# Longer query fetches, merged output stores and column-paired MLP products in a fused retention and MLP kernel

## The chip, the cores and the metric

The kernel runs on one core of one Trainium2 chip. The metric is the device time of one execution, in microseconds, given as the median of several runs. A run is called slow when it lies over 1.5% above the fastest of the same kernel; ratios leave slow runs out.

## The reference, cut to what matters

```python
# q, k, v: (8, 8, 576, 64) float32; w_in: (512, 2048); w_out: (2048, 512)
scores = (q @ k.transpose(0, 1, 3, 2)) / sqrt(64)
Dmat   = where(i >= j, gamma[h] ** (i - j), 0)          # decay, causal
attn   = (scores * Dmat) @ v                             # (8, 8, 576, 64)
x      = attn.transpose(0, 2, 1, 3).reshape(4608, 512)
h      = x @ w_in
out    = (h * clip(h + 3, 0, 6) / 6) @ w_out             # (4608, 512)
```

## The kernel before

The sequence is cut into chunks of 128 rows (four of each of eight batches) and four tail chunks, numbered 0 to 35 in order of use. The queries, keys and values of a chunk are loaded by SyncE, scaled to 16 bits by GpSimd or VectorE, and the scaled queries and keys are transposed by a DMA that ScalarE issues. TensorE then makes the chunk's scores and its part of x. When the chunks of a batch are done, the MLP runs on that block of 512 rows: TensorE makes an up product, ScalarE an activation `u` from it, VectorE `g`, and TensorE the down products, which from block 1 on are seven products in place of eight. So while block n goes through the MLP, the chunks of block n+1 go through attention, on all engines at once.

The order of everything is one long string that is worked off token by token: `l20` loads chunk 20, `c20.0g` scales its queries on GpSimd (`v` is VectorE), `x20` transposes, `s20` and `o20` are scores and output, `u3.5` is an up product and its activation, `P3.4` a down product. Each engine's list of instructions follows the order of this string, and in the trace of the kernel before each engine runs through its list in order, going by source lines: TensorE's 3,695 matmuls, VectorE's 341 instructions and SyncE's 180 DMAs without exception, and ScalarE's 294 instructions but for five transposes that begin one or two places early.

```python
COL_UP, COL_DOWN = (5, 6, 8, 7), (4, 5, 6, 8, 7)   # blocks in column pairs

def load(c, only=None):                              # three loads a chunk
    ...
    nc.sync.dma_start(st[:, ix, :, :],               # runs of 256 bytes
        src[b, :, t * P:(t + 1) * P, :].rearrange("h s d -> s h d"))

def xpose(c):
    qt = work.tile([P, 8, P], FP16, tag="qkT", bufs=4, name="qkT")
    nc.scalar.dma_start_transpose(qt, qk.rearrange("p a h d -> p (a h d)"))

def mul(ps, lhs, rhs, start, stop, halves=True):
    if not halves:
        nc.tensor.matmul(ps, lhs, rhs, ...)          # full, 128 columns
        return
    for z in range(2):                               # a column pair
        nc.tensor.matmul(ps[z * D:z * D + D], lhs[:, z * D:z * D + D], rhs, ...)

def hswish(ph, dst):                                 # ScalarE, then VectorE
    nc.scalar.activation(u, ph, ACTF.Relu, bias=0.5, scale=1.0 / 6.0)
    nc.vector.scalar_tensor_tensor(out=dst, in0=uv, in1=pv, ...)   # frees ph
# ... (product: each quarter of a block is stored as soon as it is ready)
```

Each DMA that SyncE or ScalarE issues announces its landing on a semaphore. The built program hands out eight of them in turn over all these DMAs, loads, stores and transposes alike; in the trace of the kernel before, the 208 DMAs name eight semaphores, 26 DMAs each. A DMA shares its semaphore with the one eight places earlier in that order, and its engine doesn't issue it before that one has landed: of the 200 DMAs that have such a predecessor none was issued before its landing, and the closest came 0.02 us after it. The order comes from the build's own model of how long instructions take.

Of the kernel before, what the change touches and what calls it, by code (L numbers as in the profile page):

```python
# [33 lines left out]

PROGRAM = """
# [3 lines left out]
c2.2g o2 h0.0.0.1 w0.3s c3.2g o3 h0.0.2.3 h0.1.0.1.8 w0.2g W1.0 W1.6 W1.1  # L39
W1.2 W1.3 w0.5g w0.6g l4 h0.1.2.3 l5 w0.7s W1.7 W1.4 w0.4g W1.5 u0.4 u0.5  # L40
u0.6 l6 l7 l8 w1.1g w1.6v u0.7 w1.3g u0.8 u0.9 w1.0s u0.10 u0.11 u0.12 c4.0g
u0.13 u0.14 u0.15 w1.2s c4.1g p0 w1.5s y4v c5.0g p1 c4.2g p2 w1.4g l9 w1.7s
c5.2g c5.1v y5v s4 p3 c6.0g s5 o4 c6.1g c6.2v l10 p4 l11 p5 c7.0g c7.1v
c8.0g c8.1g l12 c7.2g t0 t1 l13 c9.0g p6 y6s s6 o5 p7 y7s h1.0.0.8 c8.2g
h1.0.1.9 o6 s7 c9.1g h1.0.2.10 h1.0.3.11 c9.2v c10.0g c10.2g c10.1g x8
h1.0.4.12 l14 c11.0g c11.1g o7 h1.0.5.13 l15 x9 h1.0.6.14 c11.2g l16
h1.0.7.15 h1.1.0.8 h1.1.1.9 h1.1.2.10 h1.1.3.11 t2 c12.0g c12.1g e1.1.0.4
h1.1.4.12 l17 h1.1.5.13 h1.1.6.14 h1.1.7.15 x10 c12.2g e1.1.4.8 e1.2.0.8 s8
t3 P1.0 P1.1 x11 P1.2 P1.3 e1.3.0.8 s9 o8 x12 e1.4.0.8 l18 P1.4 o9 c13.0g
c13.2g c13.1g l19 s10 P1.5 P1.6 x13 c14.2g h2.0.0.8 c14.0g c14.1g h2.0.1.9  # L50
h2.0.2.10 h2.0.3.11 l20 h2.0.4.12 o10 x14 s11 h2.0.5.13 h2.0.6.14 o11 s12
c15.0g c15.1g c15.2g h2.0.7.15 h2.1.0.8 h2.1.1.9 c16.0g c16.1g o12 l21 s13
c17.0g c17.1g h2.1.2.10 h2.1.3.11 h2.1.4.12 e2.1.0.4 x15 c16.2g c17.2g
h2.1.5.13 h2.1.6.14 h2.1.7.15 e2.1.4.8 l22 o13 c18.0g x16 e2.2.0.8 P2.0 s14
x17 P2.1 e2.3.0.8 P2.2 c18.1g s15 o14 c19.0v c19.1g x18 c18.2g l23 P2.3 s16
c19.2g o15 c20.0g c20.1g e2.4.0.8 P2.4 s17 o16 x19 P2.5 l24 c20.2g l25 P2.6
u3.0 u3.8 s18 o17 u3.1 u3.9 x20 c21.0g c21.2g u3.2 u3.10 u3.3 u3.11 e3.3.0.4
u3.4 u3.12 e3.1.0.4 c21.1g c22.2g c22.0g l26 u3.5 l27 c22.1g l28 u3.13 x21
o18 s19 u3.6 u3.14 u3.7 u3.15 e3.1.4.8 e3.2.0.8 c23.0g s20 e3.3.4.8 o19
c23.1g P3.0 e3.4.0.8 P3.1 c24.0g P3.2 x22 P3.3 c23.2g s21 c24.1g o20 P3.4  # L60
l29 x23 c24.2g c25.0v c25.1g P3.5 P3.6 l30 c25.2g u4.0 u4.8 s22 o21 u4.1
c26.2v c26.0g c26.1g u4.9 x24 u4.2 u4.10 u4.3 o22 c27.0g u4.11 e4.3.0.4 u4.4
u4.12 l31 l32 e4.1.0.4 u4.5 u4.13 x25 s23 c27.1g u4.6 u4.14 u4.7 u4.15
e4.1.4.8 e4.2.0.8 x26 s24 o23 c27.2v l33 c28.0g c28.1v e4.3.4.8 c28.2g P4.0
P4.1 P4.2 s25 e4.4.0.8 x27 o24 c29.2g c29.0v c29.1g P4.3 l34 P4.4 P4.5 s26
o25 P4.6 u5.0 u5.8 x28 u5.1 u5.9 s27 o26 u5.2 u5.10 u5.3 u5.11 c30.0g c30.1v
c31.0g c31.1g l35 e5.1.0.4 x29 e5.3.0.4 u5.4 u5.12 u5.5 u5.13 s28 o27 u5.6
c30.2g u5.14 u5.7 u5.15 e5.1.4.8 x30 e5.3.4.8 e5.2.0.8 P5.0 P5.1 c31.2v s29
c32.2g c32.0g c32.1g o28 x31 e5.4.0.8 P5.2 c33.0g c33.1v P5.3 x32 o29 s30
P5.4 x33 P5.5 P5.6 u6.0 u6.8 u6.1 c34.0g c34.1v o30 s31 u6.9 u6.2 u6.10 s32  # L70
o31 u6.3 c33.2v u6.11 u6.4 s33 o32 x34 e6.1.0.4 u6.12 u6.5 c34.2g u6.13 u6.6
e6.3.0.4 u6.14 u6.7 u6.15 e6.3.4.8 c35.0g e6.1.4.8 e6.2.0.8 e6.4.0.8 c35.1g
x35 s34 o33 P6.0 P6.1 P6.2 P6.3 s35 o34 c35.2v P6.4 P6.5 o35 P6.6 u8.0 u8.8
u8.1 u8.9 u8.2 u8.10 u8.3 u8.11 e8.1.0.4 u8.4 u8.12 u8.5 u8.13 u8.6 u8.14
u8.7 u8.15 e8.1.4.8 e8.2.0.8 e8.4.0.8 P8.0 P8.1 P8.2 P8.3 e8.3.0.4 e8.3.4.8
P8.4 P8.5 P8.6 u7.0 u7.8 u7.1 u7.9 u7.2 u7.10 u7.3 u7.11 u7.4 u7.12 e7.1.0.4
u7.5 u7.13 u7.6 e7.3.0.4 u7.14 u7.7 u7.15 e7.1.4.8 e7.2.0.8 e7.3.4.8 P7.0
P7.1 P7.2 e7.4.0.8 P7.3 P7.4 P7.5 P7.6
# [5 lines left out]
def kernel(  # L84
# [21 lines left out]
    COL_UP, COL_DOWN = (5, 6, 8, 7), (4, 5, 6, 8, 7)  # L106
# [23 lines left out]
    NS16 = 2  # L130
    s16s = [const.tile([P, HP, P], FP16, name=f"s16_{i}") for i in range(NS16)]
# [3 lines left out]
    tq = const.tile([P, 9, H], FP32)  # L135
    tkv = const.tile([P, 9, H], FP32)
    ts = const.tile([P, HP], FP32)
    pos = const.tile([P, 9], FP32)
    etab = const.tile([P, 9, H], FP32)
    lngt = const.tile([P, H], FP32)  # L140

    stage = {}
    qk16s, qkTs, ats, xts, gs = {}, {}, {}, {}, {}
    v16s, s16_of, kns = {}, {}, {}
    cidx = {}

    def load(c, only=None):
        kind, b, t = c
        if not only:
            stage[c] = work.tile([P, 3, H, D], FP32, tag="st", bufs=6,  # L150
                                 name="st")
        st = stage[c]
        for ix, src in enumerate((q, k, v)):
            if only is not None and ix != only:
                continue
            if kind == 0:
                nc.sync.dma_start(
                    st[:, ix, :, :],
                    src[b, :, t * P:(t + 1) * P, :].rearrange("h s d -> s h d"))
            else:  # L160
                for z in range(2):
                    nc.sync.dma_start(
                        st[z * TAIL:(z + 1) * TAIL, ix, :, :],
                        src[b + z, :, MAIN:S, :].rearrange("h s d -> s h d"))

    def cast(c, ix, eng):
        kind, b, t = c
        st = stage[c]
        ti = t if kind == 0 else 4
        if ix == 2:  # L170
            v16s[c] = work.tile([P, H, D], FP16, tag="v16", bufs=5, name="v16")
        elif c not in qk16s:
            qk16s[c] = work.tile([P, 2, H, D], FP16, tag="qk16", bufs=5,
                                 name="qk16")
        dst = v16s[c] if ix == 2 else qk16s[c][:, ix, :, :]
        tab = (tq if ix == 0 else tkv)[:, ti, :]
        eng.tensor_tensor(out=dst, in0=st[:, ix, :, :],  # L177
                          in1=tab.unsqueeze(2).to_broadcast([P, H, D]),
                          op=ALU.mult)

    def xpose(c):
        qk = qk16s[c]
        qt = work.tile([P, 8, P], FP16, tag="qkT", bufs=4, name="qkT")
        qkTs[c] = qt
        nc.scalar.dma_start_transpose(
            qt, qk.rearrange("p a h d -> p (a h d)"))
        kns[c] = qk[:, 1, :, :]
# [35 lines left out]
    def xpose0(ix, p0, eng):  # L223
# [6 lines left out]
        if ix == 1 and p0 == 3:  # L230
            for t in range(NC4):
                qkTs[(0, 0, t)] = wout16[:, 0:8, t * P:(t + 1) * P]
# [13 lines left out]
    def load_v(t):  # L246
        st = work.tile([P, 3, H, D], FP32, tag="st", bufs=6, name="st")
        stage[(0, 0, t)] = st
        nc.sync.dma_start(st[:, 2, :, :], v[0, :, t * P:(t + 1) * P, :]
# [6 lines left out]
    def xpose_pe(c, tag, eng):  # L256
        qk = qk16s[c]
        qt = work.tile([P, 8, P], FP16, tag="qkT", bufs=4, name="qkT")
        qkTs[c] = qt
        kns[c] = qk[:, 1, :, :]  # L260
# [10 lines left out]
    def ret1(c, nwarm=0, two=False):  # L271
        kind, b, t = c
        qt = qkTs[c]
# [8 lines left out]
        for p in range(HP):  # L282
            for z in range(2):
                nc.tensor.matmul(sc[z][:, p, :],  # L284
                                 qt[z * D:z * D + D, HP + p, :],
                                 qt[z * D:z * D + D, p, :],
                                 start=True, stop=True)
        at = work.tile([P, 2, HP, P], FP16, tag="at", bufs=2, name="at")
        ats[c] = at
        m = mask01 if kind == 0 else maskt  # L290
# [10 lines left out]
    def ret2(c):  # L301
        kind, b, t = c
        qt, kn, at, vt = qkTs.pop(c), kns.pop(c), ats.pop(c), v16s.pop(c)
        qk16s.pop(c, None)
        xp = psum.tile([P, HP, P], FP32, tag="xp", name="xp")
        rows = [slice(0, D), slice(D, P)]
        for p in range(HP):
# [4 lines left out]
            if kind == 0 and t > 0:  # L312
                s16 = s16_of[b]
                for z in range(2):
                    nc.tensor.matmul(xp[rows[z], p, :], s16[:, p, rows[z]],  # L315
                                     qt[:, p, :], start=False,
                                     stop=(p == HP - 1), skip_group_check=True)
            elif kind == 1:
                for y in range(2):
                    cs = slice(y * TAIL, (y + 1) * TAIL)  # L320
                    for z in range(2):
                        nc.tensor.matmul(
                            xp[rows[z], p, cs], s16t[(b + y) % 4][:, p, rows[z]],
                            qt[:, p, cs], start=False, stop=(p == HP - 1),
# [34 lines left out]
    def mul(ps, lhs, rhs, start, stop, halves=True):  # L359

        if not halves:
            nc.tensor.matmul(ps, lhs, rhs, start=start, stop=stop,  # L362
                             skip_group_check=True)
            return
# [14 lines left out]
    def up(kb, fc, nwarm=0):  # L379
# [7 lines left out]
        for m in range(NCC):  # L387
            mul(ph, win16[:, m, P * fc:P * fc + P], xt[:, m, :],
                m == 0, m == NCC - 1, kb in COL_UP)
        hswish(ph, g[:, fc, :])  # L390

    def up_half(kb, hb, fcs, nwarm=0):
# [9 lines left out]
        for j, fc in enumerate(fcs):  # L402
            for m in range(NCC):
                mul(ph[:, 256 * j:256 * j + 256],
                    win16[:, m, P * fc:P * fc + P], xt[:, m, cs],
                    m == 0 and j == 0, m == NCC - 1, kb in COL_UP)
# [19 lines left out]
    def down_plain_part(kb, pos, f0, f1):  # L426
        g = gs[kb]
        for fc in range(f0, f1):
            for mc, po in enumerate(pos):
                mul(po, g[:, fc, P * mc:P * mc + P], wout16[:, fc, :],  # L430
                    fc == 0, fc == NFC - 1, kb in COL_DOWN)

    def down_plain_end(kb, pos):
        for mc, po in enumerate(pos):
            ob = work.tile([P, DM], FP32, tag="osb", bufs=4, name="osb")
            if mc % 2:
                nc.vector.tensor_copy(ob, po)
            else:
                nc.scalar.copy(ob, po)
            store(kb, mc * P, ob, 0, DM)  # L440
# [30 lines left out]
    def product(kb, name):  # L471
# [26 lines left out]
        for fc in range(HF):  # L498
            for m in range(2):
                mul(ps[:, m, :], lhs(fc, m), rhs[:, fc, :],  # L500
                    first and fc == 0 and m == 0, fc == HF - 1 and m == 1,
                    kb in COL_DOWN)
# [8 lines left out]
        else:  # L511
# [5 lines left out]
            ob = work.tile([P, 2, 256], FP32, tag="osb", bufs=4, name="osb")  # L517
            if name == "P2":
                nc.scalar.copy(ob, ps)  # L519
                i, j = 0, 0  # L520
            elif name == "P7":
                nc.vector.tensor_tensor(out=ob, in0=ps, in1=d["Z"], op=ALU.add)
                i, j = 1, 1
            elif name == "P4":
# [197 lines left out]
```

## Time and profile before

| | before |
|---|---|
| time, median of 3 runs | 305.24 us |
| span of the profiled run | 300.9 us |
| TensorE idle after 20 us, summed from the trace's records | 2.8 us |
| mean from issue to landing, loads issued after 55 us | 5.83 us |

The profiled run itself took 303.04 us.

These are the load and store queue (q1) and the transposes' queue (q10) on the page of the kernel before, with packets, megabytes and the share of the 16 DMA engines' span that the packets took:

```profile
q1 hardware_dynamic: 120128, 46.15, 70.9%
q10 hardware_dynamic: 29568, 7.34, 18.8%
```

And this is ScalarE's timeline of the kernel before around the transpose of chunk 20. A line of a timeline has the start, the duration, the engine (ACTq is ScalarE's sequencer), the source line, the operation with output and inputs, and the idle time before it with what ended it.

```profile
125.08 1.29 ACT L371 ACTIVATE u<-ph 128x512 f32<-128x512 f32 x2
125.85 1.25 ACTq L185 DMA_TRANSPOSE qkT<-qk  x1
127.20 1.75 ACT L371 ACTIVATE u<-ph 128x512 f32<-128x512 f32 x3 [0.84 <-DVE g L376]
```

ScalarE issues the transpose right behind its activations (125.85), spends 1.25 us on it and goes on. It does not stand.

### The profile page before, as it was taken

Reading aid. Unit: us, or ns where it says so; the run is one execution under the profiler, and the core shown is the slowest. Engines: PE = TensorE matmul, PEld = TensorE weight load, DVE = VectorE, ACT = ScalarE, POOL = GpSimd, SP = SyncE. Lnnn points to the kernel's source line nnn. Section 1 sums busy time; section 2 is a strip of 40 time slices with the busy share of each in tenths; the row PEclk is TensorE's granted clock in tenths of the full one; section 3 lists DMA queues with packets and bytes.
Section 4 is the critical chain, followed back from the end, with each engine's and each line's share of the span. In section 5 each row is a group of like instructions: output and inputs, shape, how many; then the busy total and the mean of one; then the engine's idle time right before and its main releaser. Section 6 shows DMA issues by size and latency. Waiting matters only on the chain.

```text
span 300.9 us, 8762 instructions
## 1 busy us (share of the span) xinstructions
PE 290.1 (96%) x3695; PEld 209.9 (70%) x3695; DVE 238.8 (79%) x341; ACT 145.0 (48%) x267; POOL 103.8 (35%) x116
## 2 busy tenths in 40 slices
PE   8889998998999999999999999999999999999994
PEld 3565454787788888547854896579757975895694
DVE  6756744989978999699778996998699768857953
ACT  2777714864237723565157423753477136306610
POOL 5254554966258635553744122334200000000000
PEclk9979999999999999999999999999999999999999
DMA  7999999999999999999999999999723130014003
GB/s 234 310 349 385 232 308 207 223 201 210 272 166 189 238 229 215 197 196 231 201 234 263 228 190 173 245 254 158 138 20 53 39 105 2 3 45 98 1 18 126
DMA packets 149735, 54.05 MB, mean 180 GB/s; under 512 B 134848, under 2 KB 145088, under 8 KB 149696
## 3 DMA queue, kind: packets, MB, share of 16 engines
q1 hardware_dynamic: 120128, 46.15, 70.9%
q10 hardware_dynamic: 29568, 7.34, 18.8%
q8 instruction: 29, 0.48, 0.7%
q14 instruction: 10, 0.08, 0.1%
HBM read 36.70 MB, written 9.44 MB: 153 GB/s over the span
## 4 chain that ended last, share of the span: by engine, by line
PE 90%; DVE 4%; ACT 3%; issue 1%
PE ph L362 22%; PE ph L366 17%; PE accB L366 6%; PE accC L366 6%; PE accA L366 6%; PE po L362 5%; PE xp L309 4%; PE accB L362 4%; PE sc L284 4%; PE accA L362 3%; PE accC L362 3%; PE accD L366 3%; PE xp L254 2%; PE xp L315 2%; DVE g L376 2%; PE accD L362 2%
## 5 line engine op out<-in xcount | busy, mean ns | idle before, releaser
L371 ACT ACTIVATE u<-ph 128x512 f32<-128x512 f32 x144 | 84.1, 597 | 62.9 <-PE ph L366 28.5
L376 DVE SCALAR_TENSOR_TENSOR g<-u,ph 128x512 f16<-128x512 f32 x144 | 94.6, 684 | 23.4 <-ACT u L371 22.2
L362 PE MATMUL ph<-xt,win 128*128 128x256 f16 (+1 forms) x464 | 72.3, 313 | 0.0
L362 PEld LDWEIGHTS <-win 128*128 128x128 f16 x464 | 44.3, 98 | 23.0
L177 POOL TENSOR_TENSOR qk<-st,tq 128x512 f16<-128x512 f32 x29 | 31.7, 1092 | 52.7 <-DMA st<-in_q_dram 23.8
L366 PEld LDWEIGHTS <-win 128*64 128x64 f16 x512 | 29.1, 110 | 24.4 <-issue 0.4
L177 POOL TENSOR_TENSOR v<-st,tkv 128x512 f16<-128x512 f32 x29 | 32.6, 1127 | 34.8 <-DMA st<-in_v_dram 16.5
L295 DVE TENSOR_TENSOR at<-sc,mask 128x1024 f16<-128x1024 f32 (+1 forms) x34 | 39.0, 1155 | 5.5 <-PE sc L284 5.4
L366 PE MATMUL ph<-xt,win 128*64 128x512 f16 x384 | 43.0, 379 | 0.2 <-DVE g L376 0.2
L366 PEld LDWEIGHTS <-ss 128*64 128x64 f16 x640 | 34.5, 110 | 0.4 <-DVE ss L464 0.3
L177 POOL TENSOR_TENSOR qk<-st,tkv 128x512 f16<-128x512 f32 x26 | 28.5, 1095 | 7.7 <-PE accA L362 5.9
L339 ACT ACTIVATE xt<-xp 128x512 f16<-128x512 f32 x32 | 19.1, 597 | 20.4 <-PE xp L315 16.0
L362 PEld LDWEIGHTS <-g 128*128 128x128 f16 x208 | 19.6, 98 | 10.4 <-issue 2.0
L366 PEld LDWEIGHTS <-g 128*64 128x64 f16 x480 | 26.1, 110 | 0.6
L464 DVE TENSOR_TENSOR ss<-g 128x1024 f16<-128x1024 f16 (+1 forms) x30 | 23.6, 798 | 0.3
L309 PE MATMUL xp<-at,v 128*64 128x128 f16 x288 | 20.8, 229 | 1.0 <-ACT xt L339 0.8
L362 PEld LDWEIGHTS <-ss 128*128 128x128 f16 x192 | 18.3, 98 | 2.9 <-DVE ss L464 0.6
L366 PE MATMUL accB<-tmat,ss 128*64 128x256 f16 x320 | 19.2, 273 | 0.0
L309 PEld LDWEIGHTS <-v 128*64 128x64 f16 x288 | 14.9, 112 | 6.1 <-issue 2.9
L366 PE MATMUL accA<-wout,g 128*64 128x256 f16 x320 | 19.1, 273 | 0.0
L519 ACT COPY osb<-accA 128x512 f32<-128x512 f32 x8 | 4.7, 586 | 28.0 <-PE accA L366 17.2
L345 ACT CAST s<-state 64x256 f16<-64x256 f32 x48 | 17.3, 361 | 0.5
(94 smaller groups left out, 319.3 us busy)
## 6 DMA issues: line engine op xcount, KB each, us to landing
st<-in_v_dram SPq DMA_DIRECT2D x32, 256.0 KB, 6.2
out_dram<-osb SPq DMA_DIRECT2D x32, 256.0 KB, 5.0
st<-in_q_dram SPq DMA_DIRECT2D x28, 256.0 KB, 5.7
st<-in_k_dram SPq DMA_DIRECT2D x28, 256.0 KB, 6.0
wst<-in_moe_w_in_dram SPq DMA_DIRECT2D x4, 512.0 KB, 7.2
tmat<-in_moe_w_in_dram SPq DMA_DIRECT2D x4, 512.0 KB, 8.0
wst<-in_moe_w_out_dram SPq DMA_DIRECT2D x4, 512.0 KB, 11.1
g<-in_moe_w_out_dram SPq DMA_DIRECT2D x4, 512.0 KB, 6.1
```

Source lines behind the costliest of these rows:

```text
L177: eng.tensor_tensor(out=dst, in0=st[:, ix, :, :], in1=tab.unsqueeze(2).to_broadcast([P, H, D]), op=ALU.mult)
L254: nc.tensor.matmul(ps, zero16[:, 0:P], zero16[:, 0:w], start=True, stop=True)
L284: nc.tensor.matmul(sc[z][:, p, :], qt[z * D:z * D + D, HP + p, :], qt[z * D:z * D + D, p, :], start=True, stop=True)
L295: nc.vector.tensor_tensor(out=dst, in0=src, op=ALU.mult, in1=m[:, :].unsqueeze(1).to_broadcast([P, n, P]))
L309: nc.tensor.matmul(xp[rows[z], p, :], vt[:, 2 * p + z, :], at[:, z, p, :], start=(p == 0), stop=False, skip_group_check=True)
L339: nc.scalar.activation(xts[b][:, :, t * P:(t + 1) * P], xp, ACTF.Copy, scale=0.125)
L345: nc.scalar.copy(s16[rows[z], :, rows[z]], sp[rows[z], :, :])
L362: nc.tensor.matmul(ps, lhs, rhs, start=start, stop=stop, skip_group_check=True)
L366: nc.tensor.matmul(ps[z * D:z * D + D], lhs[:, z * D:z * D + D], rhs, start=start, stop=stop, skip_group_check=True)
L371: nc.scalar.activation(u, ph, ACTF.Relu, bias=0.5, scale=1.0 / 6.0)
L376: nc.vector.scalar_tensor_tensor(out=dst, in0=uv, scalar=1.0, in1=pv, op0=ALU.min, op1=ALU.mult)
L464: nc.vector.tensor_tensor(out=dst, in0=a, in1=c, op=op)
```

## The change

The change has four parts. Queries of two neighbouring chunks are fetched by one DMA in runs of 512 bytes: a partition then holds rows 2p and 2p+1, so the two chunks' transposes hold queries of both and keys of both, and the scores of an even chunk need both transposes. Outputs of two chunks leave in merged stores, with runs of 2,048 bytes. All MLP products run as column pairs. And the order of the program is made anew.

```diff
-    COL_UP, COL_DOWN = (5, 6, 8, 7), (4, 5, 6, 8, 7)
...
+            if kind == 0 and ix == 0:
+                if t % 2 == 0:
+                    sq = work.tile([P, H, 2, D], FP32, tag="sq", bufs=SQ_BUFS, name="sq")
+                    stageq[pair_of(c)] = sq
+                    nc.sync.dma_start(
+                        sq.rearrange("p h r d -> p h (r d)"),
+                        src[b, :, t * P:(t + 2) * P, :]
+                        .rearrange("h (p r) d -> p h (r d)", r=2))
+                continue
...
+            if part == 0:                      # transpose of the even chunk: queries of both
+                q4 = qt.rearrange("z (r h) n -> z r h n", r=2)
+                qops[cu] = (lambda p, r_, q4=q4, u=u: q4[r_, :, p, u * 64:u * 64 + 64])
+            else:                              # of the odd chunk: keys of both
+                kops[cu] = lambda p, r_, u=u: qt[r_, u * HP + p, :]
...
-    def mul(ps, lhs, rhs, start, stop, halves=True):
-        if not halves: ...                     # the full form is gone
+    def mul(ps, lhs, rhs, start, stop):
...
-            ob = work.tile([P, 2, 256], FP32, tag="osb", bufs=4, name="osb")
+            if ("o", i) not in d:
+                d["o", i] = work.tile([P, 2, DM], FP32, tag="osb", bufs=2, name="osb")
...
+            elif name in ("P4", "P3"):         # second quarter of a half: store both
+                js = slice(0, DM)
... (PROGRAM: 40 lines, all made anew; value buffers 5 -> 6)
```

## The prediction

> **What bounds the kernel now.** I read the page of the kernel before first: its busy table, its chain and its queue table. Then the waits of TensorE alone, and then TensorE's instructions in order of time in two stretches, one where the MLP products are full matmuls and one where they already run in column pairs.
>
> ```profile
> PE 290.1 (96%) x3695; PEld 209.9 (70%) x3695; DVE 238.8 (79%) x341; ACT 145.0 (48%) x267; POOL 103.8 (35%) x116
> DMA  7999999999999999999999999999723130014003
> PE 90%; DVE 4%; ACT 3%; issue 1%
> ```
>
> TensorE is busy 96% of the 300.9 us span and is 90% of the chain that ended last. DMA is full until about 220 us, but only matters if TensorE waits for what it brings. The waits of TensorE after 20 us, where the MLP begins, are few:
>
> ```profile
> PE sc L284 <- ACT qkT L269: 1.1, 1, 1.1
> PE accA L362 <- DVE g L376: 0.8, 1, 0.8
> PE po L362 <- DVE g L376: 0.5, 1, 0.5
> PE ph L366 <- DVE g L376: 0.2, 1, 0.2
> ```
>
> That is 2.6 us, and no line names a DMA. So the end moves only if TensorE gets less to do, or does it faster. Start times in the timeline give its pace (durations overlap, so I take differences of starts). Unpaired stretch:
>
> ```profile
> 104.95 0.29 PE L334 MATMUL state<-v,qk 128*64 128x64 f16 x8
> 105.17 1.92 PE L362 MATMUL accA<-wout,g 128*128 128x256 f16 x16
> 107.02 0.40 PE L284 MATMUL sc<-qkT 64*128 64x128 f16 x8
> 107.35 1.92 PE L362 MATMUL accC<-tmat,ss 128*128 128x256 f16 x16
> ...
> 117.71 1.92 PE L362 MATMUL accD<-tmat,g 128*128 128x256 f16 x16
> 119.47 1.80 PE L362 MATMUL accC<-wout,ss 128*128 128x256 f16 x15
> ```
>
> Paired stretch:
>
> ```profile
> 170.16 1.91 PE L366 MATMUL accC<-tmat,ss 128*64 128x256 f16 x32
> 171.91 1.91 PE L366 MATMUL accB<-tmat,ss 128*64 128x256 f16 x32
> 173.75 0.40 PE L284 MATMUL sc<-qkT 64*128 64x128 f16 x8
> 174.08 0.25 PE L309 MATMUL xp<-at,v 128*64 128x128 f16 x2
> ...
> 174.55 0.29 PE L334 MATMUL state<-v,qk 128*64 128x64 f16 x8
> 174.68 1.92 PE L366 MATMUL accA<-wout,g 128*64 128x256 f16 x32
> ```
>
> What is to be seen: a product followed by another product of the same form takes 1.75 us, as 32 column halves (170.16 to 171.91) and as 16 full matmuls (117.71 to 119.47, 1.76). **Pairing as such is worth nothing.** A product followed by matmuls of another form takes 1.85 (105.17 to 107.02) or 1.84 (171.91 to 173.75): about 0.10 more. The eight state matmuls, which are column halves, take 0.22 us before a full product and 0.13 before a paired one: the same 0.1 again. Scores take 0.33 before either. So a change of form costs some 0.10 us, and pairs remove changes.
>
> [...] Weight loads of 64 columns do take 110 ns against 98 for 128 columns, but two of them hide behind each pair, as 1.75 against 1.76 us shows. [...] The median spacing of starts in this trace is 109 and 216 for full matmuls, and 2 x 108 for a pair of 512[...]. [...] on the load and store queue 256 bytes took 23 ns in the mean, 1,024 bytes 55, 2,048 bytes 92.
>
> **The change part by part.**
>
> *Column pairs.* Before, blocks 5 to 8 go up in pairs and blocks 4 to 8 down in pairs; after, all do. I walked both instruction lists of TensorE, called each matmul full, column half or row half (scores are row halves), and counted changes of form. Before: 27 full/row, 26 full/column, 43 row/column, together 96. After: 3, 8 and 57, together 68 (what is left of full ones are transposes and warming). Some of the fall comes from the order: in five places the scores of two chunks now stand back to back. 28 fewer changes x 0.10 = **-2.8 us**, all on TensorE's own path. The number of matmuls rises from 3,695 to 4,559, at a spacing (54 ns per 256-column half) that the stretch at 170 us already keeps up, beside full DMA.
>
> *Order.* The wait of 1.1 us for ScalarE's copy of a transpose stands where a chunk's scores follow its transposes directly (a transpose at 50.55, the scores at 52.26). The new order puts two steps of the plain down product between them in that place and others between later ones: **-1.1**. The other three waits (1.5 us) are the hand-over from the up products to the down products, whose order stays: 0.
>
> *Queries in 512-byte runs.* 28 loads of 1,024 packets of 256 bytes become 14 of 1,024 packets of 512. Estimated at 33 ns for 512 bytes (between 23 and 55): 28,672 x 23 = 659 us of one engine become 14,336 x 33 = 473; over 16 engines 11.6 us. *Merged stores* of six blocks and the tail block: 7,168 packets of 1,024 bytes become 3,584 of 2,048, 394 against 330, or 4 us over 16 engines. Together 16 of about 269 us of DMA time (89.7% of the span). TensorE waits for no DMA, so **0** on the path. GpSimd waits 23.8 us for queries; it is 35% busy and off the path.
>
> *Casts.* VectorE gets 30 casts of q, k and v where it had 16, GpSimd 70 for 84: 14 x 0.69 = 9.7 us more. Seven chunks' masks are done in two halves: 7 x (2 x 0.684 - 1.218) = 1.1 more, one weight cast 0.7. VectorE goes from 238.8 to about 250 us, 84% of a shorter span. From 60 to 200 us it is now 88% busy (18.6, 16.8, 18.9, 17.1, 15.7, 18.8, 17.0 in windows of 20 us). Most of the new casts fall there: about 96% by the same sum. TensorE's four product buffers come free through VectorE, so it should wait a little more: I choose **+0.8**.
>
> *Start and tail.* A mask, an iota and wider tables cost GpSimd some 0.7 us before its first cast, for which it idles 1.9 us anyway: 0. In the last block each quarter is now stored by two issues, at 0.42 us per issue in this trace, so the last data leaves 0.4 later but is half as large: **+0.2**.
>
> Sum: -2.8 - 1.1 + 0.8 + 0.2 = -2.9. From 305.24: 302.3. The order was evidently made anew as a whole, and I give it another half microsecond for small waits that I can't see: **301.8 us**.
>
> **The rivals.**
> 1. *VectorE becomes the bound.* For it: 88% busy between 60 and 200 us, and stretches where its work exceeds TensorE's. Against it: the kernel before has such stretches too (around 70 us) and loses only 0.8 us there. If lag adds up in each of six blocks at 0.8, the gain is gone: 304 to 306.
> 2. *DMA was the hidden bound.* For it: full until 220 us, GpSimd's long waits for q and v. Were the loads what paced the order of the program, lighter ones would let a tighter order through: 297 to 299. Against it: no wait of TensorE names a DMA, and in 164 to 200 us TensorE was busy 35.84 of 36.00.
> 3. *The added instructions starve TensorE*, or the strided query operand (two runs of 64 columns) streams slower. For it: only that nothing in this trace reads so. Against it: the paired stretch at full DMA. A tenth more on the score and state matmuls that read queries (some 15 us) would make 303.5.
>
> **Range and chances.** The switch term is good to about 1 us either way, the waits to 2. That gives 298.8 to 304.8 for 8 in 10. Faster by over 2% needs less than 299.1, which takes rival 2 or a much better order: 0.13. Slower by over 2% (311.3) needs a real stall: 0.03. The rest, 0.84, is within 2%.
>
> **What would show it.** Right: full MLP matmuls gone from the groups; a product 1.75 us from start to start in the stretch at 75 to 160 us; the state matmuls 0.13 before a product everywhere; no 1.1 us wait for a transpose; TensorE still at 96% or more; VectorE near 250 us; DMA busy tenths falling sooner. Wrong: waits of TensorE for VectorE's g or ss of over 3 us in sum (rival 1); any lengthening of score or state matmuls (rival 3); or a gain above 5 us that the count of switches can't pay for (rival 2).

Of the spacings of starts named in it, 109 and 216 ns belong to full matmuls of 256 and of 512 columns.

## The result and the profile after

The changed kernel took 320.0 us (median of 4 runs, 318.81 to 325.25) against 305.35 in the same rounds. It is slower by 4.7% (ratio 1.0472, 95% interval 1.0421 to 1.0523). A ratio here is the mean time of one kernel's fast runs over the mean time of the other's fast runs of the same rounds, so it is not quite the ratio of the medians that I quote.

The first profile of the changed kernel fell into a slow run. The lines below are from a second build of the same file (run e1), whose profiled run is fast: 320.64 us, ratio 1.0496, span 318.8 us. Its busy table, its PEclk line (the granted TensorE clock in tenths, 40 slices), its queues and its chain:

```profile
PE 294.5 (92%) x4559; PEld 228.1 (72%) x4559; DVE 249.1 (78%) x363; ACT 143.4 (45%) x266; POOL 92.1 (29%) x105
PEclk9979999999999989799999989999999999999999
q1 hardware_dynamic: 101920, 46.15, 64.5%
q10 hardware_dynamic: 29568, 7.34, 18.5%
PE 58%; DMA 13%; DVE 11%; SPq 8%; issue 4%; POOL 3%; ACT 2%; ACTq 1%; POOLq 0%
```

VectorE's work is what I had summed (249.1 us for about 250), the matmuls are the 4,559 that I had counted, and the DMA queues take a smaller share. But TensorE is busy for 92% of a span that is 18 us longer, and the chain that ended last, which was TensorE for 90% before, now goes through DMAs, VectorE and the issuing of DMAs (SPq is SyncE's sequencer) for a third. The waits of TensorE in the same run, with the sum, the number and the longest:

```profile
PE ph L424 <- DVE g L434: 5.5, 5, 2.5
PE xp L370 <- ACT xt L401: 3.6, 3, 2.5
PE sc L347 <- DMA qkT<-qk: 2.2, 1, 2.2
```

TensorE waits for VectorE's `g`, for ScalarE and for a transposing DMA. VectorE had time to spare (78%), so I asked what it waited for itself: ScalarE's `u`. And ScalarE was idle for 24.1 us just ahead of its 28 transposes, against 1.1 us before: partly for operands that weren't ready, partly for something else. Here is the chain that ended last in the same run, in order of time, around one of these:

```profile
118.39 9.20 DMA st<-in_k_dram
127.59 0.02 issue
...
127.75 1.25 ACTq L241
```

The chain runs from a load of keys, which lands at 127.59, to the transpose of chunk 19 that ScalarE issues at that very moment. These two share no data: what this transpose reads, the scaled queries of chunks 19 and 20, lay ready by 123.7 us. What they share is the semaphore, eight places apart. It is ScalarE that stands for it: its sequencer goes on at 127.61, 0.02 us after the landing, issues the transpose from 127.75 on, and the next activation behind it starts at 129.04.

Around three of TensorE's waits its clock fell too: the digits 8, 7 and 8 in the PEclk line, near 112, 128 and 183 us (a slice is 8 us). They follow waits of 2.5, 2.5 and 2.2 us. In this run it ran at half speed for 10.2 us after 22 us (0 before).

So the theory after the result: **A.** The places of the transposes in the rotation of semaphores have moved against the loads, and ScalarE stands for loads and stores that have nothing to do with its transposes. **B**, the rival: column pairs slow TensorE themselves, or what feeds it. **C**, another: the new order and the coupling of two chunks cost the time. **D**: the new loads and stores do.

### The profile page after: what moved, and what is told of

It is laid out like the page before. It is cut to its first block, busy times and chain, and to the rows that moved or that the text cites. A ratio compares the mean times of both kernels' runs of the same rounds, so it can differ in the third digit from the quotient of the medians.

```text
span 323.5 us, 10450 instructions
## 1 busy us (share of the span) xinstructions
PE 294.6 (91%) x4559; PEld 225.2 (70%) x4559; DVE 251.0 (78%) x363; ACT 143.1 (44%) x266; POOL 91.3 (28%) x105
## 4 chain that ended last, share of the span: by engine, by line
PE 48%; DVE 16%; DMA 16%; SPq 8%; issue 4%; POOL 4%; ACT 2%; ACTq 1%; POOLq 0%
PE ph L424 19%; PE accB L424 7%; DVE g L434 5%; PE accA L424 5%; DMA st<-in_k_dram 5%; PE accC L424 5%; DMA g<-in_moe_w_out_dram 4%; PE po L424 4%; SPq L619 3%; DMA st<-in_v_dram 3%; DVE at L356 3%; PE accD L424 3%; DVE ss L522 3%; POOL qk L211 2%; DMA qkT<-qk 2%
## 5 line engine op out<-in xcount | busy, mean ns | idle before, releaser
L424 PE MATMUL ph<-xt,win 128*64 128x512 f16 (+1 forms) x1312 | 120.1, 338 | 11.7 <-DVE g L434 11.2
L424 PEld LDWEIGHTS <-win 128*64 128x64 f16 x1440 | 83.9, 112 | 53.4 <-issue 15.4
L424 PEld LDWEIGHTS <-ss 128*64 128x64 f16 x1024 | 54.5, 110 | 4.0 <-DVE ss L522 2.6
L424 PEld LDWEIGHTS <-g 128*64 128x64 f16 x896 | 48.9, 110 | 7.3 <-issue 1.3
L211 POOL TENSOR_TENSOR qk<-sq,tq 128x512 f16<-128x512 f32 x20 | 22.1, 1107 | 63.3 <-DMA sq<-in_q_dram 17.6
L356 DVE TENSOR_TENSOR at<-sc,mask01p 128x1024 f16<-128x1024 f32 (+1 forms) x35 | 34.2, 1003 | 2.6 <-PE sc L347 2.6
L522 DVE TENSOR_TENSOR ss<-g 128x1024 f16<-128x1024 f16 (+1 forms) x30 | 23.4, 789 | 0.3
L424 PE MATMUL accC<-tmat,ss 128*64 128x256 f16 x256 | 15.7, 274 | 0.5 <-DVE ss L522 0.5
L424 PE MATMUL po<-wout,g 128*64 128x512 f16 x128 | 15.3, 381 | 0.6 <-DVE g L434 0.5
L424 PE MATMUL accC<-wout,ss 128*64 128x256 f16 x256 | 15.4, 273 | 0.1
L424 PE MATMUL accD<-tmat,g 128*64 128x256 f16 x256 | 15.4, 273 | 0.0
```

Of the source, the lines that this page charges most:

```text
L211: eng.tensor_tensor(out=dst, in0=src, in1=tab.unsqueeze(2).to_broadcast([P, H, D]), op=ALU.mult)
L356: nc.vector.tensor_tensor(out=dst, in0=src, op=ALU.mult, in1=m[:, :].unsqueeze(1).to_broadcast([P, n, P]))
L522: nc.vector.tensor_tensor(out=dst, in0=a, in1=c, op=op)
```

## The experiments

"Before" is the kernel before of the same rounds. In the table, *stood* is ScalarE's idle time just ahead of its 28 transposes in the profiled run; *of it rotation* counts those cases alone in which the DMA eight places earlier landed at most 0.25 us before the issue. *PE waits* is TensorE's idle time after 20 us, *half clock* the time at half speed between 22 us and the last 3 us. Half clock counts while TensorE waits, too: in e5, 10.4 of its 13.7 us lie within one wait. The profile in the row "before" is that of the run of 303.04 us. All profiled runs are fast but that of e10, whose trace I don't use for times.

| run | us | before | ratio (95%) | stood, of it rotation | PE waits | half clock |
|---|---|---|---|---|---|---|
| before (first profile) | 305.24 | | | 1.1, 1.1 | 2.8 | 0 |
| e1 changed kernel again | 320.64 | 306.41 | 1.0496 (1.0429-1.0562) | 24.1, 10.4 | 14.4 | 10.2 |
| e2 before + all pairs | 316.27 | 306.41 | 1.0329 (1.0265-1.0393) | 15.4, 15.0 | 14.2 | 6.8 |
| e3 new code, old order | 342.41 | 306.41 | 1.1170 (1.1096-1.1243) | 11.2, 11.2 | 32.6 | 17.1 |
| e4 old code, new order | 317.55 | 306.41 | 1.0373 (1.0301-1.0446) | 11.8, 0.0 | 13.8 | 7.3 |
| e5 before, other DMA places | 324.83 | 306.01 | 1.0630 (1.0559-1.0701) | 21.3, 21.3 | 21.2 | 13.7 |
| e6 e2 with e5's places | 331.77 | 306.01 | 1.0860 (1.0791-1.0928) | 27.6, 26.9 | 26.9 | 23.9 |
| e7 pairs from block 3 on | 312.80 | 306.01 | 1.0225 (1.0138-1.0312) | 12.6, 11.7 | 11.5 | 0 |
| e8 changed, pairs from block 3 on | 322.05 | 306.01 | 1.0552 (1.0470-1.0634) | 15.8, 0.0 | 14.3 | 10.2 |
| e9 e7, transposes earlier | 313.34 | 306.66 | 1.0165 (1.0105-1.0225) | 3.4, 2.3 | 12.0 | 3.4 |
| e10 before, no pairs | 305.42 | 306.66 | 0.9968 (0.9918-1.0018) | (slow run) | | |
| e11 e3 with before's pairs | 323.66 | 306.66 | 1.0575 (1.0520-1.0631) | 0.3, 0.0 | 19.8 | 6.8 |
| e12 before, transposes on SyncE | 320.67 | 305.21 | 1.0524 (1.0481-1.0567) | none | 15.7 | 13.7 |
| e13 e12 + all pairs | 326.63 | 305.21 | 1.0703 (1.0657-1.0750) | none | 21.7 | 17.1 |
| e15 e8, one transpose earlier | 316.10 | 305.21 | 1.0365 (1.0323-1.0407) | 10.6, 0.3 | 13.0 | 0 |
| e16 e15, stores not merged | 319.73 | 306.35 | 1.0498 (1.0421-1.0574) | 13.2, 1.8 | 14.5 | 6.8 |
| e17 e15, query runs of 256 bytes | 324.46 | 306.35 | 1.0641 (1.0559-1.0723) | 15.0, 1.7 | 17.9 | 4.4 |

All gave correct results.

**e1, the changed kernel once more.** No edit.

> The changed kernel once more, for fast executions and a profile in the fast state. All theories: about 319 us (318.8 to 320.2 in its fast executions so far), ratio 1.045 to 1.05. If the profile is of the fast state, TensorE's waits should sum to some 18 us against 6.6 of the kernel before; the waits for VectorE's g and for ScalarE's xt should stay the longest groups.

It confirmed the result and gave the fast profile shown above.

**e2, column pairs alone.** The kernel before, and nothing but:

```diff
-    COL_UP, COL_DOWN = (5, 6, 8, 7), (4, 5, 6, 8, 7)
+    COL_UP, COL_DOWN = tuple(range(9)), tuple(range(9))
```

> The kernel before with all MLP products in column pairs, nothing else. Step of my prediction: 26 changes of form fewer at 0.10 us each, so 302 to 303.5 us. Theory columns (the 864 added matmuls or the lost full form slow TensorE beside full DMA): 310 us or more.

316.27 us: the pairs alone cost 3.3%, some 10 us. (The 26 fewer changes of form were a miscount: the built program has 79 for 96, 17 fewer.) The instruction lists of the other four engines are the same as before, one by one. ScalarE's timeline of e2 at the same transpose of chunk 20:

```profile
131.92 1.09 ACT L371 ACTIVATE u<-ph 128x512 f32<-128x512 f32 x2
137.26 1.80 ACTq L185 DMA_TRANSPOSE qkT<-qk  x1
139.16 2.06 ACT L371 ACTIVATE u<-ph 128x512 f32<-128x512 f32 x4 [6.15 <-issue]
```

And TensorE's timeline of e2 in that stretch, with three windows of the same run (length; then busy time and count of PE, PEld, DVE, ACT and POOL; granted clock; DMA share; GB/s):

```profile
133.39 1.92 PE L366 MATMUL ph<-xt,win 128*64 128x512 f16 x16 [0.41 <-DVE g L376]
140.53 6.46 PE L366 MATMUL ph<-xt,win 128*64 128x512 f16 x32 [5.22 <-DVE g L376]
```

```profile
130.00:140.00 10.00, 3.83 (x32) 2.17 (x32) 3.82 (x6) 3.80 (x9) 4.31 (x5) 0.97 1.32 218
140.00:147.00 7.00, 6.47 (x40) 3.60 (x41) 5.32 (x9) 3.02 (x6) 0.00 (x0) 0.55 1.36 209
```

Between 133.0, where the last activation of the first line ends, and 137.26 ScalarE does nothing; the bracket counts up to the next activation and so includes the issue. The operands of chunk 20 had been ready since 121.8 us. The load of keys eight places earlier landed at 137.2 us. Behind the transpose four activations wait, TensorE's four product buffers stay full, TensorE stands for 5.22 us, and then the same products take twice as long for some 6 us because the clock is at half (0.55 in the window; it fell 4.1 us into the wait and stayed there for 6.8 us). In the kernel before, the DMA eight places earlier had landed well before 25 of the 28 transposes; in e2 the landing was what released 9 of the 28, and TensorE, at most 1.3 us behind the kernel before up to 107 us, was 14.2 us behind at its chunk of 133 us and 14.0 us behind at the end. The new pairs stand in blocks 0 to 4, so if they were slow of themselves, it would show before 107 us too. Nearly all of the loss falls where ScalarE stood 14.9 us for the transposes of chunks 15 to 20.

**e3 and e4, layout and order apart.** e3 is the changed code with the order of before (five tokens moved so that both chunks of a pair are there); e4 is the code of before with the new order. e4 needs its own chunk's queries where the new order has them later, so 23 of its scalings had to be moved, and it took the sixth value buffer.

> The changed kernel's code (query pairs, merged stores, column pairs) under the order of the kernel before; only five steps are moved, as far as the pairs demand it. Theory order (the new order puts casts and transposes that wait for late loads ahead of the draining of product buffers in the in-order queues of VectorE and ScalarE): 301 to 306 us. Theory layout (pairs of queries and merged stores tie two chunks together and make loads late whatever the order): 314 to 322 us.

> The kernel before's code (single loads, small stores, its column sets) under the order of the changed kernel; from the 13th chunk on, 23 casts are delayed because the old layout has no buffers for them so early. Theory order: 313 to 322 us. Theory layout: 303 to 308 us.

Neither is near the kernel before: 342.41 and 317.55 us. In e3 ScalarE stood 11.2 us for the rotation, and TensorE waited 22.0 us for transposes: the scores of an even chunk now need the odd chunk's transpose as well, which the old order brings a chunk too late. e4 has no such transpose at all: nothing stands for the rotation, and TensorE waits most for GpSimd:

```profile
PE xp L309 <- POOL v L177: 6.1, 3, 2.8
```

These are values that GpSimd scales too late, partly because of the scalings that I had to move. So e4 shows that the new order isn't good for the old code; it doesn't size the order for the new.

**e5 and e6, other places in the rotation.** The only edit makes the build take another of its models of time when it puts the DMAs in order. The instructions of all five engines and their order are unchanged (compared one by one; eight of them wait for another engine at a slightly different place).

```diff
-    with _tile.TileContext(nc) as tc:
+    with _tile.TileContext(nc, schedule_with_timeline_sim=True) as tc:
```

The number of loads and stores that stand ahead of a transpose in the build's order, for some chunks:

| | x8 | x12 | x16 | x20 | x24 | x28 |
|---|---|---|---|---|---|---|
| before | 43 | 59 | 77 | 92 | 115 | 139 |
| e2 | 45 | 63 | 84 | 102 | 125 | 147 |
| e7 | 43 | 59 | 77 | 92 | 118 | 142 |
| e5 | 63 | 74 | 95 | 112 | 130 | 148 |
| e6 | 64 | 74 | 97 | 114 | 130 | 148 |

> The kernel before, with the same instructions in the same order on all five engines (compared one by one); the only edit makes the build use another model of time when it puts the DMAs in one order, so that each DMA gets another of the eight completion semaphores in rotation, and the transposes x8 to x30 stand 8 to 22 places later among the loads and stores. Theory A (a transpose on ScalarE's queue waits until the DMA eight places ahead of it in that order has landed, and ScalarE stands meanwhile): clearly slower than 305, 315 to 340 us, with ScalarE idle ahead of the transposes and TensorE waiting for VectorE's g. Rival B (column pairs slow TensorE or its clock of themselves, DMA places don't matter): 304 to 307 us, since nothing of the pairs is changed.

> All products in column pairs and otherwise the kernel before, built with the same other model of time as e5, so that its DMA places are nearly those of e5 (at most two places apart). Theory A: the same as e5 or up to 3 us shorter, since the pairs are now all that differs. Rival B: about 10 us longer than e5, as e2 was 10 us longer than the kernel before.

e5 took 324.83 us: the same instructions, 6.3% longer, through the places alone. Its chain shows how, at the first transpose:

```profile
72.14 3.67 DMA out_dram<-osb
75.81 0.02 issue
...
75.89 1.40 ACTq L185
...
77.39 0.61 ACT u L371
...
78.02 0.70 DVE g L376
...
78.76 1.25 PE ph L362 x5
```

A *store* of finished outputs lands and with that releases a *transpose* of operands, then come `u`, `g` and TensorE. ScalarE stood 13.7 us for it. TensorE waited 12.9 us, and the window behind reads, as above:

```profile
68.40:82.00 13.60, 3.24 (x16) 2.31 (x17) 3.49 (x7) 3.15 (x6) 4.18 (x5) 0.50 1.25 245
```

The granted clock is 0.50 for the whole of it, from 2.5 us into the wait to 3 us behind it. The gaps of 5.22 us (e2) and 12.9 us (e5) were followed by half clock, and so were shorter ones: gaps of 2.47, 2.54 and 2.16 us (e1), 2.06 us (e4) and 1.81 us (e16), each for 3.4 us. Gaps of 2.28 us (e15) and 2.41 us (e5, at 145 us) were not. So in these runs a gap of about 2 us was already a risk, and no length between 1.81 and 2.41 us tells the two cases apart.

e6 was to be at most 3 us shorter than e5 and was 7 us longer, so this expectation failed. Two of its transposes stand two places later than in e5, x16 and x20 (x8, x9, x15 and x17 one place). Exactly there ScalarE stood 4.1 us (0.1 in e5) and 5.5 us (2.4), and behind the second TensorE waited 5.4 us and fell to half clock for 6.8 us. So e6 did not hold the places equal, and can't separate A from B. It shows how sharp the edge is: two places decide whether ScalarE stands for 0.1 or for 4.1 us.

**e7 and e9, pairs from block 3 on.**

```diff
-    COL_UP, COL_DOWN = (5, 6, 8, 7), (4, 5, 6, 8, 7)
+    COL_UP, COL_DOWN = (3, 4, 5, 6, 7, 8), (3, 4, 5, 6, 7, 8)
```

> The kernel before with column pairs in blocks 3 to 8 (up products of blocks 3 and 4 and down products of block 3 are new), which leaves every DMA place up to the transpose of chunk 21 as before and moves later ones by at most 4. Theory A: 302 to 306 us. Rival B (a cost of each product in pairs): three of the nine half blocks that e2 changed are changed here, a third of its 10 us: 308 to 310 us.

e7 took 312.80 us and met neither range. Up to chunk 21 the places are those of before, and ScalarE hardly stood there. But three or four places later were enough from chunk 24 on: it stood 4.0, 2.7 and 2.9 us ahead of transposes 26, 28 and 29, and TensorE's longest waits follow, 1.8 and 1.6 us for `g` from 195.1 and 203.8 us on. These explain a part only. At 121 us, ahead of its first product that differs, e7's TensorE is already 5.6 us behind the first profile of the kernel before, and 10.3 us behind at the end. The first part can't come from the pairs; since that profile is of a fast run, much of it may be the spread between runs. I then moved the transposes of chunks 22 to 30 two to five steps earlier in the order (e9), which brings their places back.

> e7 (column pairs from block 3 on) with the transposes of chunks 22 to 30 written 2 to 5 steps earlier in the program and one load one step later; this brings the places of all transposes among the DMAs back to those of the kernel before (equal or up to 3 earlier, but for chunk 27 which is 2 later). The casts of these chunks were done 8 to 18 us ahead of the transposes in e7, so the earlier transposes don't wait for data. Theory A (the places in the rotation of semaphores cost e7 its 7 us): the idle time of ScalarE ahead of transposes 24 to 29 (12 us in e7) goes below 3 us and the time to 303 to 307 us. Rival B (the products in pairs are themselves slower where attention runs beside them): 311 to 314 us, as e7.

ScalarE's standing fell to 3.4 us as expected, but not the time: the fast runs lie between 310.0 and 314.2 us. An earlier transpose is also issued earlier, so that the DMA eight places ahead is again just landing: seven transposes were released by it, if only after a short wait. And the issue itself took longer, 1.68 us in the mean against 1.44, thus 28 x 0.24 = 6.7 us more of ScalarE's time. TensorE's longest wait, 3.0 us at 167 us with half clock for 3.4 us behind it, again lies at such a transpose: that of chunk 25, whose operands had been ready for 11 us, was issued 0.08 us after the landing eight places earlier and took 2.49 us to issue. So e9 did not remove what theory A blames, and it speaks neither for A nor clearly for B.

**e8, the changed kernel without the early pairs.** The same two sets of blocks as in e7, put into the changed kernel.

> The changed kernel with the products of blocks 0 to 2 in full form as before and column pairs from block 3 on; its transposes come 1 to 11 places earlier in the order of DMAs. Theory A: the waits of ScalarE ahead of the transposes of chunks 10 to 19 shrink and the time falls by 5 to 12 us to 308 to 315. Rival B: pairs in blocks 3 and 4 still cost a third; 313 to 317. Rival C (the merged stores and the new order are what costs): 318 to 321, as the changed kernel.

322.05 us, no gain. (The built program's transposes come 1 to 5 places earlier, not 1 to 11.) The rotation no longer holds any transpose (10.4 us before that), but ScalarE stood 15.8 us ahead of transposes whose operands weren't there yet, and one wait weighs most. TensorE's timeline of e8:

```profile
172.72 4.27 PE L429 MATMUL ph<-xt,win 128*64 128x512 f16 x38
181.36 0.61 PE L348 MATMUL sc<-qkT 64*128 64x128 f16 x8 [4.37 <-DMA qkT<-qk]
```

The scores of chunk 24 wait 4.37 us for the transpose of chunk 25, its partner, which holds the keys of both; and from 2.6 us into that wait on TensorE's clock is at half for 6.8 us. That is theory C in one place.

**e10, no pairs at all.** Both sets empty.

> The kernel before with no column pairs at all: 110 changes of TensorE's form in place of 96, and places of the transposes equal to those of before up to chunk 27, then 2 earlier. Theory A with 0.10 us a change: 1.4 us longer than before, 306 to 308. Rival B (pairs cost time of themselves): the pairs of blocks 4 to 8 are gone, so faster than before, 300 to 303.

305.42 us, ratio 0.9968 (0.9918 to 1.0018): the same as before. Fourteen more changes of form (110 for 96) cost nothing to be seen, where 0.10 us each would be 1.4 us; the interval leaves room for some 0.5 us. The pairs of blocks 4 to 8 don't cost anything worth naming either.

**e11, layout without new pairs in the old order.** e3 with the column sets of before.

> e3 (the changed kernel's loads, transposes and merged stores in the order of the kernel before, 342 us) with the column pairs of the kernel before instead of pairs everywhere; its transposes of chunks 10 to 16 come 1 to 4 places later than before, not 3 to 8 as in e3. Theory A: most of e3's loss goes; 308 to 320 us. Rival D (the new loads and stores cost the time themselves): 335 us or more.

323.66 us, in between, so 19 us below e3 and over the range of A. ScalarE hardly stands now (0.3 us, none of it for the rotation), but:

```profile
PE sc L348 <- DMA qkT<-qk: 11.9, 5, 4.1
```

TensorE waits five times, 11.9 us in all, for the partner's transpose. In the kernel before it never does.

**e12 and e13, transposes off ScalarE.** `nc.scalar.dma_start_transpose` becomes `nc.sync.dma_start_transpose`. All DMAs are then on one queue, in the order of the program, and e13 differs from e12 in TensorE's products alone (checked on the instruction lists of all engines and on the order of the DMAs).

> The kernel before with its 28 DMA transposes issued by SyncE, at their places in the program among the loads and stores, instead of by ScalarE. All DMAs are then on one queue and their order is the program's, whatever the model of time. Theory A: ScalarE has 40 us less of issuing and never stands for a transpose; the time is 301 to 309 us (SyncE may stand for casts and delay loads behind). No rival is tested by this run alone; it is the base for the next.

> All products in column pairs, transposes issued by SyncE: the order of all DMAs and all engines' streams are those of e12, and only TensorE's products differ. Theory A (pairs cost time only through the places of the transposes): within 2 us of e12, rather 1 to 2 us shorter for 17 fewer changes of form. Rival B (pairs cost time of themselves beside attention): 8 to 12 us longer than e12, as e2 against before.

e12 was no improvement as a kernel: with the 28 transposes on SyncE the kernel before takes 15 us longer (320.67 for 305.21). SyncE stands for operands and stores ahead of a transpose (the first one was issued behind stores that SyncE held until their data was ready), and TensorE waits for the transposes. The places of the DMAs changed too (58 loads and stores ahead of x8 in place of 43), so the issuing engine and the places are not told apart. The wait lines of e12 and of e13:

```profile
PE sc L284 <- DMA qkT<-qk: 13.7, 4, 6.3
```

```profile
PE sc L284 <- DMA qkT<-qk: 19.4, 4, 8.0
```

But e13 is 6 us longer than e12, so theory A isn't the whole. The 5.7 us are in these waits. From 67 us on, the loads and with them the transposes come about 2 us later in e13, and 4 to 5 us later by 160 us. I see two traces of a reason. With pairs, more instructions are fetched: q8, which the page calls an instruction queue, moved 35 packets of 16 KB for 29, as it did in e2 against the kernel before, where only TensorE's list is longer (4,559 matmuls for 3,695). And over all eighteen traces a load's issue between 45 and 220 us took 1.13 us in the mean (1,434 of them), but 1.71 us (247) when such a packet began between 0.3 us before and 0.9 us after its start; in two of the traces (e3, e15) there is no such difference. Six more packets would add 6 x 0.6 = 3.6 us to the issuing, not all of it on the path. This is a correlation; I made no kernel that changes the fetches alone.

**e15, the late transpose mended.** e8 with `x25` five activations earlier and a fifth buffer for transposed operands, without which it could not run there.

```diff
-... u4.9 u4.2 u4.10 ... s23 x25 o22 ...
+... u4.9 x25 u4.2 u4.10 ... s23 o22 ...
-        qt = work.tile([P, 8, P], FP16, tag="qkT", bufs=4, name="qkT")
+        qt = work.tile([P, 8, P], FP16, tag="qkT", bufs=5, name="qkT")
```

> e8 (changed kernel, pairs from block 3 on) with the transpose of chunk 25 written five activations earlier and a fifth buffer for transposed operands so that it can run there. Theory C (what is left of the loss is the pair coupling: scores of an even chunk wait for the partner's late transpose, 4.4 us at 176 us, then 6.8 us at half clock): that wait and the half clock go, 314 to 318 us. Rival: another wait takes its place, 320 to 323.

316.10 us, within theory C's range, and ratio 1.0365 for e8's 1.0552: one token and one buffer are worth 6 us of the changed kernel's loss. TensorE's longest wait for a transpose is now 1.2 us, and the half clock is gone.

**e16 and e17, the layout's two parts.** e16 is e15 with each quarter stored at once (`if kb < B:` in place of `if kb == LAST_BLK:`); e17 is e15 with

```diff
-                    nc.sync.dma_start(
-                        sq.rearrange("p h r d -> p h (r d)"),
-                        src[b, :, t * P:(t + 2) * P, :].rearrange("h (p r) d -> p h (r d)", r=2))
+                    for r in range(2):
+                        nc.sync.dma_start(sq[:, :, r, :],
+                            src[b, :, t * P:(t + 2) * P, :]
+                            .rearrange("h (p r) d -> r p h d", r=2)[r])
```

> e15 with every quarter of a block of outputs stored as soon as it is ready (1024-byte runs, 8 stores a block in place of 4) instead of merged pairs of quarters (2048-byte runs). If the merged stores hold up the loads beside them: loads land in below 6.2 us (6.6 in e15) and the time falls by 3 us or more, below 313. If they are neutral, as predicted: 314 to 318. If the 28 more DMAs matter through the places of the transposes (up to 13 later): above 318.

> e15 with the queries of a pair of chunks fetched by two DMAs of 256-byte runs to the same places in the buffer, instead of one DMA of 512-byte runs: the same bytes and layout, 14,336 more packets of 256 bytes. At 23.7 ns against 34.2 ns per 512 bytes that is some 190 us of the 16 engines' time, 12 us of each. If the loads are on the path: 3 us or more longer, above 319. If 512-byte runs are neutral, as predicted: 314 to 318, apart from the places, which are up to 21 later.

By the ratios, undoing the merged stores costs 1.3% (1.0498 for 1.0365) and undoing the long runs 2.8% (1.0641), some 4 and 8 us. So both parts of the layout are good for the changed kernel, the long runs clearly, and theory D falls. Why they are good is not shown. Each undoing also adds DMAs (in the built programs 24 in e16, not 28, and 14 in e17), so the places move (up to 20 and 14 later, not 13 and 21), but the rotation held ScalarE for 1.8 and 1.7 us only. The 12 us of DMA time that the expectation of e17 counted did not come: the packets' sum over 16 engines was 275.1 us, for 276.0 in e15. What the trace of e17 does show is that TensorE's longest wait, 4.2 us at 188 us, goes back through ScalarE's transposes and GpSimd's scalings to a load of queries that landed at 185.3 us.

No version of these beats the kernel before; e10 equals it.

## Why the prediction was wrong, point by point

**"-2.8 us, all on TensorE's own path"** is the step that failed first. The count was right (68 changes; pairs alone have 79), a product still takes 1.75 us (160.63 less 158.88 in e1's timeline), and the state matmuls do stand 0.13 us before a product (154.65 to 154.79). So what I said of TensorE holds. What I took for granted is that the other engines wait for what they waited for before. The term measured +10 us in e2 (1.0329 x 306.41 less 306.41), with 14.2 us of waits and 6.8 us of half clock in place of 2.8 and 0. Of its causes, the rotation is shown as able to do this (e5: 21.3 us of standing and 19 us of time, with no instruction changed) and seen doing it in e2 (15.0 us, in the stretch where the time is lost). That it need not be all of it is shown by e13, 6 us longer than e12 at equal places. What these 6 us are stays open. Even the gain itself is in doubt: e10 changed the form 14 times more and lost nothing.

**"Order: -1.1"** failed. The wait of 1.1 us for ScalarE's transpose copy is still there in e1, ahead of `xp` instead of `sc`, and the new order brought waits of its own: e8 and e15 show 6 us at a single transpose, e4 shows it slow with the old code.

**"TensorE waits for no DMA, so 0 on the path"** was true of the kernel before and was the wrong thing to read. The change made DMAs matter: even chunks came to need their partner's transpose (11.9 us of waits in e11), and transposes came to wait for landings. In that kernel fetching queries in one DMA of 512-byte runs is worth some 8 us (e17), through loads on the path if not through less DMA time. The size of the saving in DMA time was nearly right for queries: from the packets of the fast profile (e1), 256 bytes took 23.4 ns before and 23.2 after and 512 bytes took 35.4, where I had estimated 33. For merged stores it wasn't. I had taken the 92 ns of the 2,048-byte packets as my basis, but 4,096 of those 4,608 packets were loads of weights. In e1 the 4,096 store packets of 2,048 bytes took 116.6 ns, as long as two of 1,024 bytes before (56.4 each), so merging saved nothing here. Packets of this one size differ, too: those of stores took 84.5 ns between 100 and 120 us and 148.1 ns between 280 and 300 us, for a cause that is not shown. The sum over the 16 engines was 267.8 us after for 272.8 before, 5 us in place of 16. Loads landed later, 6.58 us after issue for 5.83.

**"Casts: +0.8"**: VectorE did 249.1 us of work as summed. TensorE's waits for `g` were larger, 5.5 us, but not for want of VectorE; ScalarE's late `u` was behind them. Rival 1 would have been read from the same line of the waits, and would have been wrong: the engine named last is not the one that is short.

**Start and tail, +0.2**: nothing in the runs contradicts it. (In the first profile of the changed kernel GpSimd's tables and masks were done at 4.95 us, for 4.34 before, and its first cast began at 6.57 for 6.22.) **Rival 3** had its sign right for the time and the place wrong: score and state matmuls are no slower, and what more instructions may do (the fetches of e13, a correlation) would be done on the DMA queues. **"Slower by over 2% needs a real stall: 0.03"** was the worst judgement. The order is tuned so closely that 2.8 us of TensorE's waits remain in 280; such an order has more ways to get worse than to get better, and I gave a change that makes all of it anew three chances in a hundred to do so.

## What to carry to other kernels

A stream of one engine that is shown to be as fast in another form doesn't make the kernel as fast (a product took 1.75 us in either form, and e2 was 3.3% longer): build both, and compare the semaphores and places that the build hands out. ScalarE, which here also issues DMAs, stood 21.3 us in e5 for DMAs that merely shared a semaphore with its transposes. When two pieces of work are fetched together, ask which consumer now needs both, and give it room in the order and in the buffers before counting the saved packets. And when an engine with time to spare is named in a wait, follow the chain back until a transfer or an engine is reached that was itself late.
